# Block 0 of a four-layer kernel: V begun with one token tile on half the contraction, its weights loaded by quarters, two token tiles turned by DMA

## The chip, the cores and the metric

The kernel runs on one core of one Trainium2 chip. The metric is the device time of one execution in microseconds. "PE" is the TensorE matmul queue.

## The reference, cut to what matters

Four layers run in sequence on x (2048 tokens by 1024): attention, gated MLP, attention, gated MLP, each with a LayerNorm before it and a residual. An attention token looks at itself and at seven tokens at distances 2, 4, ... 14. The arithmetic is bf16.

```python
x = x + _A_ref(_layernorm(x), A_wqkv, A_wo)          # S = 2048, D = 1024, 32 heads
x = x + _B_ref(_layernorm(x), B_W_gate, B_W_up, B_W_down)   # F = 3584, relu(gate) * up
x = x + _A_ref(_layernorm(x), A_wqkv, A_wo)
x = x + _B_ref(_layernorm(x), B_W_gate, B_W_up, B_W_down)
```

The kernel works in blocks of 512 tokens, four token tiles of 128 each. Block 0's first stage is the one at issue: load x, normalise it, transpose it (the kernel's matmuls take the dimension that is summed over on the partitions, so normalised x is wanted with the 1024 channels there, as eight chunks `kc` of 128), and multiply by the V weights, then by the Q and K weights. At the start of the program TensorE has nothing to do until the first x and the first weights are there.

## The kernel before: what the change touches

V of block 0 is computed chunk by chunk of its output channels. Each accumulation runs over the whole contraction (`kc` 0 to 7), first for the tokens of tiles 0 and 1 and later for tiles 2 and 3. So the first matmul group needs a slab of V weights of 1 MB that spans all of the contraction.

```python
def v_first(ln):
    plan = [(c, 0, 2) for c in range(6)] + [(c, 2, 4) for c in range(6)] + [(c, 0, 4) for c in range(6, KC)]
    ...
            acc = psum.tile([P, BLK], F32, tag="acc", name="acc_v")
            for kc in range(KC):
                mm(acc[:, cols], lhsT=slab[("v0", c // 4)][:, kc, (c % 4) * P:(c % 4 + 1) * P],
                   rhs=ln["xnT"][:, t0:t1, kc, :], start=(kc == 0), stop=(kc == KC - 1))
            ...
            if i in ln["later"]:
                ln["later"][i]()        # PE transposes of tiles 2 and 3, inside V
```

All four tiles are transposed on TensorE, eight 128 by 128 transposes each, and copied from PSUM, the memory into which the matmuls write:

```python
hold["later"] = {2: (lambda: (turn(2), copy(2, "a", 0), copy(2, "v", 1))),
                 4: (lambda: (turn(3), copy(3, "v", 0), copy(3, "a", 1)))}
```

Nearly every transfer goes through one helper, and each is told to follow the one before it, so SyncE issues them in program order. If one of them has to wait, for data or for a free buffer, all that come after it wait too (in the profile before, the queue stood so once for 6.8 us):

```python
def sp_dma(dst, src, transpose=False):
    start = nc.sync.dma_start_transpose if transpose else nc.sync.dma_start
    if tail_sp[0] is None:
        tail_sp[0] = start(dst, src).ins
    else:
        with tc.issue_after(tail_sp[0]):
            tail_sp[0] = start(dst, src).ins
```

Weights come as slabs of 1 MB into a ring of five buffers, in the order V, V, Q, Q, K, K for block 0. A Q slab and a K slab each hold half of the contraction for all output chunks, so the first K product needs both K slabs. The sixth slab, the second one of K (called "the second K slab" below), must wait until the first V slab's buffer is free. Block 0's Q and K products alternate:

```python
QK_FIRST = [(nm, c) for c in range(KC) for nm in ("q", "k")]
```

## Time and profile before

| | before |
|---|---|
| time, median of 3 | 1619.28 us (1619.16 to 1619.67) |
| first V matmul | 9.83 us |
| first Q matmul of block 0 | 24.67 us |
| first Q matmul of block 1 | 52.30 us |
| gate's first matmul (the first MLP) | 191.08 us |

The span in the profile is about 1.7 us shorter than the time. First the page of the kernel before: span, busy times, and the chain that ended last.

```profile
span 1617.5 us, 18722 instructions
PE 1608.1 (99%) x7505; PEld 784.1 (48%) x7554; DVE 1138.3 (70%) x963; ACT 475.8 (29%) x971; POOL 176.1 (11%) x164
...
PE 99%; DMA 0%; issue 0%; SPq 0%; DVE 0%; DVEq 0%
```

TensorE is busy 99% of the span and the chain is made of it. What could be won is at the two ends. The wait table of PE, before (waiter, what it waited for, us in total, times, longest):

```profile
PE scratch L132 <- DVE ones L290: 1.5, 1, 1.5
PE acc_v L132 <- DMA w_v<-in_A_wqkv_dram: 0.9, 1, 0.9
PE tp L358 <- DVE xn_first L106: 0.7, 1, 0.7
PE tp L358 <- DVE mean L106: 0.4, 1, 0.4
```

These four are all that the table lists for PE, and they lie before the first V matmul. ("scratch" is a set of matmuls on a tile of ones that fills the start.) The chain of waits of the kernel before, in order of time (start, us, what), shows what the first V matmul hangs on:

```profile
2.20 7.59 DMA w_v<-in_A_wqkv_dram
...
9.83 2.79 PE acc_v L132 x24
```

The first V slab was issued at 2.20 us and landed at 9.79; from there on the chain is PE alone. The timeline of PE, before (start, us, engine, line, operation, output<-inputs, count, idle before):

```profile
9.83 2.79 PE L132 MATMUL acc_v<-xnT_first,w_v 128*128 128x256 bf16 x24 [0.86 <-DMA w_v<-in_A_wqkv_dram]
...
24.67 1.89 PE L132 MATMUL acc_q<-xnT_first,w_qk_q 128*128 128x512 bf16 x8
26.40 1.89 PE L132 MATMUL acc_k<-xnT_first,w_qk_k 128*128 128x512 bf16 x8
...
52.30 10.95 PE L132 MATMUL acc_q<-xnT_a,w_qk_q 128*128 128x512 bf16 x50
```

The K products begin with the group at 26.40 us. Its fifth matmul, the first to need the second K slab, is due half a group later, at about 27.26 us, and in the trace that slab landed at 26.83. So 0.4 us of slack was there. Last, the transfers in one-microsecond windows, before (window, PE busy and matmuls, granted clock, mean busy share of the DMA engines, GB/s):

```profile
13.00:14.00 1.00, 1.00 (x12) 1.00 1.04 383
14.00:15.00 1.00, 1.00 (x15) 1.00 1.06 389
15.00:16.00 1.00, 1.00 (x14) 1.00 1.04 385
16.00:17.00 1.00, 1.00 (x12) 1.00 1.06 389
```

While weights stream in, the core moves 381 to 389 GB/s without a break (12 to 19 us). The DMA engines are the second resource of this stretch, and they are full: their mean busy share in these windows is 1.02 to 1.08.

### The profile page before, as it was taken

Reading aid. Unit: us, or ns where it says so; the run is one execution under the profiler, and the core shown is the slowest. Engines: PE = TensorE matmul, PEld = TensorE weight load, DVE = VectorE, ACT = ScalarE, POOL = GpSimd, SP = SyncE. Lnnn points to the kernel's source line nnn. Section 1 sums busy time; section 2 is a strip of 40 time slices with the busy share of each in tenths; the row PEclk is TensorE's granted clock in tenths of the full one; section 3 lists DMA queues with packets and bytes.
Section 4 is the critical chain, followed back from the end, with each engine's and each line's share of the span. In section 5 each row is a group of like instructions: output and inputs, shape, how many; then the busy total and the mean of one; then the engine's idle time right before and its main releaser. Section 6 shows DMA issues by size and latency. Waiting matters only on the chain.

```text
span 1617.5 us, 18722 instructions
## 1 busy us (share of the span) xinstructions
PE 1608.1 (99%) x7505; PEld 784.1 (48%) x7554; DVE 1138.3 (70%) x963; ACT 475.8 (29%) x971; POOL 176.1 (11%) x164
## 2 busy tenths in 40 slices
PE   9999999999999999999999999999999999999999
PEld 6646544444444445444454444544445444444444
DVE  6999979996989698929489293893939939311211
ACT  4853311131116313603136031361313311131110
POOL 2300100010003002300053000530005100000000
PEclk9999999999999999999999999999999999999999
DMA  9868867697669767794747948479574884755452
GB/s 295 184 197 251 213 173 244 182 213 206 209 189 216 202 183 216 188 248 144 229 160 202 240 152 230 153 203 254 160 231 155 207 240 156 209 171 167 155 169 66
DMA packets 408440, 317.92 MB, mean 197 GB/s; under 512 B 166432, under 2 KB 389024, under 8 KB 407840
## 3 DMA queue, kind: packets, MB, share of 16 engines
q1 hardware_dynamic: 407776, 316.13, 69.4%
q8 instruction: 59, 0.97, 0.2%
q10 hardware_dynamic: 576, 0.59, 0.1%
q14 instruction: 29, 0.24, 0.1%
HBM read 266.29 MB, written 34.66 MB: 186 GB/s over the span
## 4 chain that ended last, share of the span: by engine, by line
PE 99%; DMA 0%; issue 0%; SPq 0%; DVE 0%; DVEq 0%
PE acc_u L132 24%; PE acc_g L132 24%; PE dacc L132 18%; PE acc_v L132 7%; PE acc_q L132 7%; PE acc_k L132 7%; PE acc_wo L132 7%; PE dacc_pair L132 6%; DMA w_v<-in_A_wqkv_dram 0%; PE tp L358 0%; SPq L121 0%; PE L L132 0%; DVE x L778 0%; SPq L118 0%; DVEq L1017 0%
## 5 line engine op out<-in xcount | busy, mean ns | idle before, releaser
L132 PE MATMUL acc_g<-xnT_b,w_g 128*128 128x512 bf16 x1792 | 423.3, 379 | 0.0
L132 PE MATMUL acc_u<-xnT_b,w_u 128*128 128x512 bf16 x1792 | 423.3, 379 | 0.0
L731 ACT ACTIVATE r<-acc_g 128x512 bf16<-128x512 f32 x224 | 133.6, 596 | 728.7 <-PE acc_g L132 703.8
L106 DVE TENSOR_TENSOR hT<-acc_u,r 128x512 bf16<-128x512 f32 x224 | 151.0, 687 | 243.3 <-PE acc_u L132 240.8
L132 PE MATMUL dacc<-w_d,hT 128*128 128x512 bf16 (+1 forms) x1372 | 300.4, 375 | 1.5
L132 PEld LDWEIGHTS <-hT 128*128 128x128 bf16 x1820 | 178.1, 98 | 209.0
L132 PEld LDWEIGHTS <-w_g 128*128 128x128 bf16 x1792 | 175.4, 98 | 211.4
L132 PEld LDWEIGHTS <-w_u 128*128 128x128 bf16 x1792 | 175.3, 98 | 211.4
L106 DVE TENSOR_TENSOR pv<-a,vhm 128x4096 bf16<-128x4096 bf16 x64 | 143.6, 2285 | 0.0
L778 DVE TENSOR_TENSOR x<-dacc,x 128x512 bf16<-128x512 f32 (+1 forms) x38 | 24.5, 673 | 154.1 <-PE dacc L132 154.1
L549 DVE TENSOR_TENSOR t<-q,k 128x2048 f32<-128x2048 bf16 x56 | 128.0, 2292 | 6.7 <-ACT k L485 4.6
L106 DVE TENSOR_TENSOR t<-q,k 128x2048 f32<-128x2048 bf16 x56 | 127.5, 2287 | 3.9 <-ACT k L485 2.4
L106 DVE TENSOR_TENSOR pv<-pv 128x1024 bf16<-128x1024 bf16 (+1 forms) x128 | 113.8, 952 | 0.0
L132 PE MATMUL acc_wo<-w_o,oT 128*128 128x512 bf16 x498 | 111.1, 379 | 0.7
L249 POOL TENSOR_TENSOR st_b<-st_b,neg_half 128x1 f32<-128x1 f32 x29 | 43.8, 1517 | 609.9 <-ACT st_b L248 609.9
L562 DVE TENSOR_TENSOR ac<-ac,t 128x2048 f32<-128x2048 f32 x48 | 109.7, 2285 | 0.3
L106 DVE TENSOR_TENSOR ac<-ac,t 128x2048 f32<-128x2048 f32 x48 | 109.7, 2285 | 0.0
L490 POOL COPY kh<-k 128x14 bf16<-128x14 bf16 x40 | 53.7, 1348 | 506.5 <-ACT k L485 410.4
L132 PE MATMUL dacc_pair<-w_d,hT 128*128 128x512 bf16 x413 | 95.5, 379 | 0.4
L132 PEld LDWEIGHTS <-oT 128*128 128x128 bf16 x512 | 50.1, 98 | 60.4
L244 ACT ACTIVATE xn_b<-x 128x1024 bf16<-128x1024 bf16 x29 | 30.3, 1047 | 128.6 <-DVE x L106 66.5
L410 ACT CAST vT<-acc_v 128x512 bf16<-128x512 f32 x56 | 32.7, 586 | 54.0 <-PE acc_v L132 54.0
(131 smaller groups left out, 1226.8 us busy)
## 6 DMA issues: line engine op xcount, KB each, us to landing
w_g<-in_B_W_gate_dram SPq DMA_DIRECT2D x56, 1024.0 KB, 7.2
w_u<-in_B_W_up_dram SPq DMA_DIRECT2D x56, 1024.0 KB, 5.5
w_d<-in_B_W_down_dram SPq DMA_DIRECT2D x48, 1024.0 KB, 6.0
w_o<-in_A_wo_dram SPq DMA_DIRECT2D x16, 1024.0 KB, 6.6
vhm<-v_d SPq DMA_DIRECT2D x32, 284.0 KB, 6.7
v_d<-vT SPq DMA_DIRECT2D x8, 1024.0 KB, 9.0
oT<-o_d SPq DMA_DIRECT2D x32, 256.0 KB, 4.5
w_d<-in_B_W_down_dram SPq DMA_DIRECT2D x16, 512.0 KB, 3.7
```

Source lines behind the costliest of these rows:

```text
L106: tail_dve[0] = f(*args, **kwargs).ins
L132: tail_pe[0] = nc.tensor.matmul(*args, **kwargs).ins
L244: nc.scalar.activation(xn, xt[:], ACT.Square, accum_out=sq)
L249: nc.gpsimd.tensor_tensor(rstd, vpe, neg_half[:, 0:1], op=ALU.pow)
L410: tail_act[0] = nc.scalar.copy(st["vT"][:, c, :], acc[:]).ins
L490: nc.gpsimd.tensor_copy(khalo[n][:, c, :], k[:, BLK:BLK + HALO])
L549: nc.vector.tensor_tensor(t[:], i0, i1, op=ALU.mult)
L562: nc.vector.tensor_tensor(o, ac[:], t[:], op=ALU.add)
L731: tail_act[0] = nc.scalar.activation(rs[j][:], acc[:], ACT.Relu).ins
L778: run = dv if n < NB - 2 else (lambda f, *args, **kwargs: f(*args, **kwargs))
```

## The change

Its intent is to start V earlier. V's first products take tile 0 alone and the first half of the contraction, so they need one tile of x and 1 MB of weights that comes in two quarters on two queues, ahead of x tile 3. Then V is widened: tile 1 on the first half, tiles 0 and 1 on the second half, and the same for tiles 2 and 3. The transposes of tiles 2 and 3 leave TensorE and go through the DMA. To make room, block 0 computes the first Q chunks before the first K chunk (q0 q1 q2 k0 q3 k1 ...), which brings K two groups (3.46 us) later. The diff, cut to its core (the LayerNorm statistics are dealt out anew among the engines, not shown):

```diff
+    def wv_half(hh):
+        return wqkv_v[:, hh * (KC // 2):(hh + 1) * (KC // 2), 2 * D:3 * D]
+
+    def load_slab(key, src):
+        ...
+        if key[0] == "v0":
+            for i in range(2):
+                rows = slice(i * (KC // 4), (i + 1) * (KC // 4))
+                if key[1] == 0 and i == 1:
+                    nc.scalar.dma_start(tv[:, rows, :], src[:, rows, :])
+                else:
+                    sp_dma(tv[:, rows, :], src[:, rows, :])
+        else:
+            sp_dma(tv, src)
@@ LayerNorm of block 0
-        hold["later"] = {2: (lambda: (turn(2), copy(2, "a", 0), copy(2, "v", 1))),
-                         4: (lambda: (turn(3), copy(3, "v", 0), copy(3, "a", 1)))}
+        def turn_dma(t):
+            return lambda: sp_dma(hold["xnT"][:, t, :, :], xna[:, t, :], True)
+        hold["turns"] = [turn_dma(2), turn_dma(3)]
@@ V of block 0
+        def head():
+            for kc in range(KC // 2):
+                if kc == KC // 2 - 1:
+                    ln["second"]()          # tile 1: PE transposes and copies
+                for c in range(KC):
+                    prod(kc, c, 0, 1)       # 128 x 128 times 128 tokens
+        ...
+        tail = [(GRP * (2 + 4 * part + 0.5 * i), second_half(i, 2 * part)) for part in range(2) for i in range(KC // 2)]
+        return head, [(GRP, first_half(1)), (4 * GRP, first_half(2)), (5 * GRP, first_half(3))] + tail
@@ Q and K
-        order = QK_FIRST if n < NB else QK_ORDER
+        order = QK_STAGED if staged else QK_ORDER
@@ order of events
-    ev.append((0.35, lambda: load_x(1)))
+    ev.append((0.05, lambda: load_x(0, [TPB - 1])))
+    ev.append((0.25, head))
+    spread(ln_a[0]["turns"], 0.26, 0.01)
+    ev.append((0.35, lambda: load_x(1, [0, 1])))
+    ev.append((0.45, lambda: load_x(1, [2, 3])))
@@ later events follow the K order, by two groups
-    ev.append((t_v2 + 3.2 * GRP, lambda: head_mm(0)))
+    ev.append((t_v2 + 5.2 * GRP, lambda: head_mm(0)))
```

The place of the two DMA transposes in SyncE's order is behind the first Q slab, ahead of the second Q slab, the x tiles of block 1 and both K slabs.

More of the change, by code (lines that the diff above doesn't have):

```diff
@@ L169, with load_x @@
         x_tiles.append(xt)
-    def load_x(b):
-        for t in range(b * TPB, (b + 1) * TPB):
+    def load_x(b, tiles=range(TPB)):
+        for t in (b * TPB + i for i in tiles):
             if t == 0:
@@ L179, in load_x @@
                 sp_dma(x_tiles[t][:], x_dram[t * P:(t + 1) * P, :])
-    load_x(0)
+    load_x(0, range(TPB - 1))
     slab = {}
@@ L192, in want_v, with want_v_first @@
             want((key, g), wqkv_v[:, :, 2 * D + g * SLAB:2 * D + (g + 1) * SLAB], mid if g == 0 else end)
+    def wv_half(hh):
+        return wqkv_v[:, hh * (KC // 2):(hh + 1) * (KC // 2), 2 * D:3 * D]
+    def want_v_first(end0, end1):
+        for hh, end in enumerate((end0, end1)):
+            want(("v0", hh), wv_half(hh), end)
     def want_qk(key, q_end, k_end):
@@ L213, in want_down @@
             want(("d", n, half, s), wd_v[:, rows, half * SLAB:(half + 1) * SLAB], at + gap * min(8 * (s + 1), FC))
+    def load_slab(key, src):
+        shp = list(src.shape)
+        t = wring.tile([P, 8 * SLAB], BF16, tag="slab", name="w_" + "_".join(str(k) for k in key))
+        tv = t[:, 0:shp[1] * shp[2]].rearrange("p (a b) -> p a b", b=shp[2])
+        if key[0] == "v0":
[7 more added lines that the diff above has]
+            sp_dma(tv, src)
+        slab[key] = tv
     def slab_events(events):
         for i, (key, src, _) in enumerate(slab_plan):
-            def f(key=key, src=src):
-                shp = list(src.shape)
-                t = wring.tile([P, 8 * SLAB], BF16, tag="slab", name="w_" + "_".join(str(k) for k in key))
-                tv = t[:, 0:shp[1] * shp[2]].rearrange("p (a b) -> p a b", b=shp[2])
-                sp_dma(tv, src)
-                slab[key] = tv
+            if key in slab:
+                continue
             ends = sorted(end for _, _, end in slab_plan[:i])
-            events.append((ends[i - RING] + 0.3 if i >= RING else 0.1 * i, f))
+            events.append((ends[i - RING] + 0.3 if i >= RING else 0.1 * i, lambda key=key, src=src: load_slab(key, src)))
     def ln_steps(n, which, early=False, dve=()):
@@ L287, in ln_dve_stats @@
         return mv, rstd
+    load_slab(("v0", 0), wv_half(0))
     ones = const.tile([P, SLAB], BF16, name="ones")
@@ L313, in small @@
             return stat_pool.tile([P, 1], F32, tag="f" + name, name=name, bufs=bufs)
-        mean, vpe, rstd, bst = {}, {}, {}, {}
+        mean, rstd, bst, sq = {}, {}, {}, {}
         def bn(t, half):
@@ L324, in aggr @@
             on("v", nc.vector.bn_aggr, mv[:], bst[t][:].rearrange("p a b -> p (a b)"))
-            vpe[t], mean[t] = small("vpe1"), mv[:, 0:1]
-            on("v", nc.vector.tensor_scalar, vpe[t][:], mv[:, 1:2], EPS, None, op0=ALU.add)
-            power(t)
-        def power(t):
-            rstd[t] = small("rstd1")
-            on("g", nc.gpsimd.tensor_tensor, rstd[t][:], vpe[t][:], neg_half[:, 0:1], op=ALU.pow)
-        def act_stats(t):
-            st1 = stat_pool.tile([P, 2], F32, tag="st1", name="st1")
-            on("a", nc.scalar.activation, xna[:, t, :], x_tiles[t][:], ACT.Identity, accum_out=st1[:, 0:1])
-            on("a", nc.scalar.activation, xna[:, t, :], x_tiles[t][:], ACT.Square, accum_out=st1[:, 1:2])
-            return st1
@@ L339, in act_vpe, with power, act_square @@
-        def act_vpe(t, st1):
+            mean[t] = mv[:, 0:1]
+            power(t, mv[:, 1:2], 1.0)
+        def power(t, var, sign):
+            rstd[t], vpe = small("rstd1"), small("vpe1")
+            on("g", nc.gpsimd.tensor_scalar, vpe[:], var, sign, EPS, op0=ALU.mult, op1=ALU.add)
+            on("g", nc.gpsimd.tensor_tensor, rstd[t][:], vpe[:], neg_half[:, 0:1], op=ALU.pow)
+        def act_square(t):
+            sq[t] = small("sq1")
+            on("a", nc.scalar.activation, xna[:, t, :], x_tiles[t][:], ACT.Square, scale=float(D) ** -0.5,
+               accum_out=sq[t][:])
@@ L340, in act_vpe, with act_mean, act_power @@
+        def act_mean(t):
             mn = small("mean1")
-            on("v", nc.vector.tensor_scalar, mn[:], st1[:, 0:1], 1.0 / D, None, op0=ALU.mult)
+            on("a", nc.scalar.activation, xna[:, t, :], x_tiles[t][:], ACT.Identity, scale=1.0 / D, accum_out=mn[:])
+            mean[t] = mn[:]
+        def act_power(t):
             nvar = small("nvar1")
-            on("v", nc.vector.scalar_tensor_tensor, nvar[:], st1[:, 0:1], mn[:], st1[:, 1:2], op0=ALU.mult, op1=ALU.subtract)
-            vpe[t], mean[t] = small("vpe1"), mn[:]
@@ L345, in act_vpe, with apply @@
-            on("v", nc.vector.tensor_scalar, vpe[t][:], nvar[:], -1.0 / D, EPS, op0=ALU.mult, op1=ALU.add)
-            power(t)
-        def apply(t):
-            on("v", nc.vector.tensor_scalar, xna[:, t, :], x_tiles[t][:], mean[t], rstd[t][:],
+            on("v", nc.vector.scalar_tensor_tensor, nvar[:], mean[t], mean[t], sq[t][:], op0=ALU.mult, op1=ALU.subtract)
+            power(t, nvar[:], -1.0)
+        def apply(t, half=None):
+            cols = slice(0, D) if half is None else slice(half * SLAB, (half + 1) * SLAB)
+            on("v", nc.vector.tensor_scalar, xna[:, t, cols], x_tiles[t][:, cols], mean[t], rstd[t][:],
@@ L354, in turn @@
         def turn(t):
-            tps[t] = [psum.tile([P, KC // 2, P], BF16, tag="acc", name=f"tp{h}") for h in range(2)]
+            if t == 0:
+                tps[t] = [psum.tile([P, KC // 2, P], BF16, tag="acc", name=f"tp{h}")[:] for h in range(2)]
+            else:
+                both = psum_l.tile([P, 2, KC, P], BF16, tag="L", name="tp_pair")
+                tps[t] = [both[:, h, 0:KC // 2, :] for h in range(2)]
             for c in range(KC):
@@ L362, in copy @@
             f = nc.vector.tensor_copy if eng == "v" else nc.scalar.copy
-            on(eng, f, hold["xnT"][:, t, h * (KC // 2):(h + 1) * (KC // 2), :], tps[t][h][:])
+            on(eng, f, hold["xnT"][:, t, h * (KC // 2):(h + 1) * (KC // 2), :], tps[t][h])
+        def turn_dma(t):
+            return lambda: sp_dma(hold["xnT"][:, t, :, :], xna[:, t, :], True)
         warm = small("warm")
         on("a", nc.scalar.activation, warm[:], ones[:, 0:1], ACT.Identity)
-        scratch(14)
+        scratch(13)
         bn(0, 0)
@@ L370, in ln_first, with second @@
         aggr(0)
+        act_square(2)
         bn(1, 0)
+        apply(0, 0)
+        apply(0, 1)
+        turn(0)
+        copy(0, "a", 0)
         bn(1, 1)
         aggr(1)
-        st1 = act_stats(2)
-        apply(0)
-        turn(0)
-        apply(1)
-        copy(0, "a", 1)
-        copy(0, "a", 0)
-        turn(1)
-        act_vpe(2, st1)
-        copy(1, "v", 0)
-        copy(1, "a", 1)
-        bn(3, 0)
-        bn(3, 1)
-        apply(2)
-        aggr(3)
-        apply(3)
-        hold["later"] = {2: (lambda: (turn(2), copy(2, "a", 0), copy(2, "v", 1))),
-                         4: (lambda: (turn(3), copy(3, "v", 0), copy(3, "a", 1)))}
+        copy(0, "v", 1)
+        apply(1, 0)
+        apply(1, 1)
+        act_mean(2)
+        act_power(2)
+        def second():
+            turn(1)
+            copy(1, "v", 0)
+            copy(1, "v", 1)
+            apply(2)
+            act_square(3)
+            act_mean(3)
+            act_power(3)
+            apply(3)
+        hold["second"] = second
+        hold["turns"] = [turn_dma(2), turn_dma(3)]
         return hold
@@ L416, in v_first @@
         st = att[0]
-        plan = [(c, 0, 2) for c in range(6)] + [(c, 2, 4) for c in range(6)] + [(c, 0, 4) for c in range(6, KC)]
-        def f_(i, c, t0, t1):
-            def f():
-                if i == 0:
-                    st["vT"] = big_tile([P, KC, BLK], "vT_0", True)
-                acc = psum.tile([P, BLK], F32, tag="acc", name="acc_v")
-                cols = slice(t0 * P, t1 * P)
-                with pe_group():
-                    for kc in range(KC):
-                        mm(acc[:, cols], lhsT=slab[("v0", c // 4)][:, kc, (c % 4) * P:(c % 4 + 1) * P],
-                           rhs=ln["xnT"][:, t0:t1, kc, :], start=(kc == 0), stop=(kc == KC - 1))
-                tail_act[0] = nc.scalar.copy(st["vT"][:, c, cols], acc[:, cols]).ins
-                if i in ln["later"]:
-                    ln["later"][i]()
-            return f
@@ L434, in v_first, with prod @@
-        at, out = 0.0, []
-        for i, (c, t0, t1) in enumerate(plan):
-            out.append((at, f_(i, c, t0, t1)))
-            at += GRP * (t1 - t0) / TPB
-        return out
+        pairs, opened = {}, set()
+        def prod(kc, c, t0, t1):
+            part = t0 // 2
+            if (part, c // 2) not in pairs:
+                pairs[part, c // 2] = psum.tile([P, 2, BLK // 2], F32, tag="acc", name="acc_v")
+            acc = pairs[part, c // 2][:, c % 2, (t0 % 2) * P:(t0 % 2 + t1 - t0) * P]
+            with pe_group():
+                mm(acc, lhsT=slab["v0", kc // (KC // 2)][:, kc % (KC // 2), c * P:(c + 1) * P],
+                   rhs=ln["xnT"][:, t0:t1, kc, :], start=(part, c // 2) not in opened, stop=(kc == KC - 1),
+                   skip_group_check=True)
+            opened.add((part, c // 2))
@@ new lines, in head, with first_half, second_half, f @@
+        def head():
+            st["vT"] = big_tile([P, KC, BLK], "vT_0", True)
+            for kc in range(KC // 2):
[3 more added lines that the diff above has]
+                    prod(kc, c, 0, 1)
+        def first_half(t):
+            def f():
+                for c in range(KC):
+                    for kc in range(KC // 2):
+                        prod(kc, c, t, t + 1)
+            return f
+        def second_half(i, t0):
+            def f():
+                for c in (2 * i, 2 * i + 1):
+                    for kc in range(KC // 2, KC):
+                        prod(kc, c, t0, t0 + 2)
+                tail_act[0] = nc.scalar.copy(st["vT"][:, 2 * i:2 * i + 2, t0 * P:(t0 + 2) * P],
+                                             pairs.pop((t0 // 2, i))[:]).ins
+            return f
@@ L447 @@
     khalo = {}
-    QK_FIRST = [(nm, c) for c in range(KC) for nm in ("q", "k")]
+    QK_STAGED = [(nm, c) for c in range(KC) for nm in ("q", "k")]
     QK_ORDER = [("q", 0), ("q", 1)]
@@ L855 @@
     t_gu0 = t_fill + GRP * (4 * KC - ahead)
-    want_v("v0", t_v0 + GRP * 5, t_qk0)
+    want_v_first(t_v0 + GRP * 6, t_qk0)
     want_qk("qk01", t_qk1 + GRP * KC, t_v1)
@@ L861 @@
     want_wo(0, t_fill, t_fill)
-    for at, f in v_first(ln_a[0]):
-        ev.append((t_v0 + at, f))
-    ev.append((0.35, lambda: load_x(1)))
-    ev.append((t_v0 + GRP * 5 + 0.6, lambda: load_x(2)))
-    ev.append((t_v0 + GRP * 5 + 0.7, zero_v))
+    head, steps = v_first(ln_a[0])
+    place(steps, t_v0)
+    ev.append((0.05, lambda: load_x(0, [TPB - 1])))
[3 more added lines that the diff above has]
+    ev.append((0.45, lambda: load_x(1, [2, 3])))
+    ev.append((t_v0 + GRP * 6 + 0.6, lambda: load_x(2)))
+    ev.append((t_v0 + GRP * 6 + 0.7, zero_v))
     stats, apply, turn, ln_a[1] = ln_steps(1, "a", True, range(TPB))
@@ L874 @@
     spread(qk_steps(0, ln_a[0], "qk01"), t_qk0, GRP)
-    spread(prod_sum_steps(0), t_qk0 + 3.5, 4.4)
+    spread(prod_sum_steps(0), t_qk0 + GRP * K_STEP[0] + 1.8, 4.4)
     spread(load_v_steps(0), t_qk0 + 19.0, 1.0)
@@ L885 @@
     spread(v_steps(2, ln_a[2], "v123", True), t_v2, GRP)
-    ev.append((t_v2 + 3.2 * GRP, lambda: head_mm(0)))
-    spread(softmax_steps(0), t_v2 + 3.3 * GRP, 0.01)
-    t_pv0 = t_v2 + 2.2 * GRP + 10.0
+    ev.append((t_v2 + 5.2 * GRP, lambda: head_mm(0)))
+    spread(softmax_steps(0), t_v2 + 5.3 * GRP, 0.01)
+    t_pv0 = t_v2 + 4.2 * GRP + 10.0
     spread(pv_steps(0), t_pv0, 4.3)
```

## The prediction

> **What bounds the kernel now.** TensorE. The page gives PE 1608.1 us busy of 1617.5, and the chain that ended last is 99% PE. The wait table shows four PE waits: 1.5 us for the warm-up operand, 0.7 and 0.4 us before the transposes of tiles 0 and 1, 0.9 us for the first V weights. From the first useful matmul (9.83 us) PE runs without a gap worth naming. So a change in block 0 can gain only by starting V earlier or by taking PE work out of the stretch from 9.83 us to the first Q matmul (24.67 us); it can lose by opening a gap.
>
> **What sets 9.83 us.** The first V weights, issued at 2.20 us, land at 9.79: 1 MB behind 1 MB of x in one queue, at 350 to 390 GB/s.
>
> **What the change does.**
> 1. V needs only x of tile 0 and the first half of the contraction (1 MB, in quarters on two queues, ahead of x tile 3). By the one-microsecond windows, the 1.8 MB needed have moved near 7.9 us. [...] The LayerNorm path (statistics end 5.03, two GpSimd operations of about 0.57 us, half applies of 0.3 us, four transposes, a 0.59 us copy) gives xnT's first half near 7.7 us. V starts at about 7.9 us.
> 2. V costs 4 x 1.8 us (32 matmuls of 128 columns at 56 ns, the spacing of the transposes in the trace) plus 2 x 3.45 us (256 columns at 109 ns): 14.1 us against 13.8. The transposes of tiles 2 and 3 (0.9 us) leave PE; tile 1's (0.45 us) move inside V.
> 3. New waits. Tile 1's transposes stand in PE order and wait for its apply (about 9.65 us): 0.4 us. Tiles 2 and 3 go by DMA: a DMA transpose lands 3.1 to 3.8 us after issue on a quiet queue, later behind weights. I expect tile 2 at 15 to 16 us (needed at 15.9), tile 3 at 17.5 (needed at 17.7): 0 to 0.7 us.
>
> Sum: 7.9 + 14.55 + 0.4 + 0.3 = 23.15 us to the first Q matmul, against 24.67: 1.5 us won.
>
> **Kept or lost later?** The new Q/K order brings K chunk 0 two groups (3.46 us) later; the VectorE chain moves with it, and so does the score matmul. VectorE has no idle worth naming from 36 to 184 us, so it loses 3.46 us of slack against PE: before, the last block-0 transpose for the gate stage lands near 187.5 us and gate starts at 191.08, 3.6 us of slack. I allow 0.1 us of loss.
>
> **Prediction:** 1617.8 us, range 1616.6 to 1619.3. Faster by over 2%: 0.005; within 2%: 0.99; slower: 0.005.
>
> **What would show it.** First V matmul near 7.9 us; a PE gap under 0.6 us at tile 1's transposes; 128-column V matmuls 56 ns apart; first Q near 23.2 us; gate's first matmul near 189.6 us with no idle before it.
>
> **What would make it wrong.** DMA transposes landing after 18 us; the second K slab (about 28.1 us, needed about 29) late; VectorE late at the score matmul or at gate, where slack is under 0.5 us; the weights quarter on the second queue late.

V's start of 7.9 us rests on the bytes in the one-microsecond windows of the kernel before and on the LayerNorm path. What the trace of the kernel before shows is that x tiles 1 and 2, issued on two queues at 1.26 and 1.25 us, landed at 4.73 and 4.95. That V's two quarters, on two queues, would land as early as the bytes alone say (near 7.9 us) was the estimate.

## The result

| | before | after |
|---|---|---|
| time, median of 6 | 1619.34 us (1619.16 to 1619.81) | 1619.94 us (1619.55 to 1620.90) |
| first V matmul | 9.83 | 8.37 |
| first Q matmul of block 0 | 24.67 | 23.78 |
| second K slab landed | 26.83 | 30.54 |
| first Q matmul of block 1 | 52.30 | 52.22 |
| gate's first matmul | 191.08 | 191.01 |

The ratio of after to before is 1.0004, with a 95% interval of 0.9991 to 1.0017: the same, and not the 1.5 us faster that was predicted. A ratio here is the mean time of one kernel's fast runs over that of the other's in the same rounds, so it isn't quite the ratio of the medians. The time lies above the predicted range, which ended at 1619.3.

The page of the kernel after:

```profile
span 1618.0 us, 18848 instructions
...
PE 98%; DMA 1%; issue 0%; DVE 0%; SPq 0%; DVEq 0%
```

The DMA now has a share of the chain. The wait table of PE, after:

```profile
PE scratch L132 <- DVE ones L310: 1.5, 1, 1.5
PE acc_v L132 <- DMA w_v<-in_A_wqkv_dram: 0.6, 1, 0.6
PE acc_k L132 <- DMA w_qk_k<-in_A_wqkv_dram: 0.6, 1, 0.6
PE acc_v L132 <- DMA xnT_first<-xn_first: 0.4, 1, 0.4
```

Two waits are gone (those for the transposes of tiles 0 and 1) and two are new, both for transfers: one for the DMA transposes, and one for K weights. The chain of waits, after:

```profile
1.74 6.58 DMA w_v<-in_A_wqkv_dram
...
8.37 1.51 PE acc_v L132 x24
...
11.61 5.04 DMA xnT_first<-xn_first
...
16.70 3.76 PE acc_v L132 x64
...
20.48 10.06 DMA w_qk_k<-in_A_wqkv_dram
...
30.59 1.08 PE acc_k L132 x4
```

Before, the chain left the DMA at 9.79 us for good. Now it comes back to it twice. The last time, PE's V products free a ring buffer at 20.46, the second K slab is issued at 20.48 and lands 10.06 us later, and PE goes on at 30.59. The timeline of PE, after:

```profile
8.37 1.51 PE L132 MATMUL acc_v<-xnT_first,w_v 128*128 128x128 bf16 x24 [0.63 <-DMA w_v<-in_A_wqkv_dram]
...
10.17 6.12 PE L132 MATMUL acc_v<-xnT_first,w_v 128*128 128x128 bf16 x72
16.70 7.24 PE L132 MATMUL acc_v<-xnT_first,w_v 128*128 128x128 bf16 x96 [0.41 <-DMA xnT_first<-xn_first]
23.78 5.34 PE L132 MATMUL acc_q<-xnT_first,w_qk_q 128*128 128x512 bf16 x24
28.96 1.03 PE L132 MATMUL acc_k<-xnT_first,w_qk_k 128*128 128x512 bf16 x4
30.59 1.08 PE L132 MATMUL acc_k<-xnT_first,w_qk_k 128*128 128x512 bf16 x4 [0.60 <-DMA w_qk_k<-in_A_wqkv_dram]
...
52.22 10.96 PE L132 MATMUL acc_q<-xnT_a,w_qk_q 128*128 128x512 bf16 x50
```

The idle times in brackets understate the loss, because the ends of matmuls are modelled: a group of eight is shown with 1.89 us, though the next one starts 1.73 us after it. Counted in starts of matmuls, there are three waits. The products on tile 1 were due at 10.62 us and began at 10.85, 0.23 late, because VectorE was still copying tile 1's transposes out of PSUM (the first of its two copies ended at 10.79; no bracket shows this wait). The products on tile 2 were then due at 16.124 and began at 16.698, 0.57 late. The K group's fifth matmul was due at 29.82 (28.96 plus half a group of 1.73) and began at 30.59, 0.77 late. The sum is then:

- V begins 1.46 us earlier (9.83 to 8.37).
- V takes 0.57 us longer up to the first Q matmul (14.84 to 15.41). Waits make up 0.80 of its time: 0.23 for tile 1's copies and 0.57 for tile 2. So 0.89 us is won at the first Q matmul.
- The wait for the second K slab takes 0.77 of that back, and 0.04 goes in small steps. At block 1's first Q matmul 0.08 us is left (52.30 to 52.22).
- From there on PE runs alike: gate at 191.01 against 191.08 with no idle before it, and the last matmul group starts 0.04 us earlier than before (1613.01 against 1613.05).

The profiled span is nonetheless 0.44 us longer, and that is the last store of the output: in the trace it took 2.17 us to land (at 1616.86) against 1.61 us (at 1616.24). No edit of the change is at that store, but it does not look like chance: over all fourteen profiles it took 2.17 to 2.33 us in the six kernels that have both a quarter of V on ScalarE's queue and tiles 2 and 3 moved by SyncE (after, a0, e2, e3, b2, c2), and 1.56 to 1.61 us in the other eight. Why is not shown.

The windows show why the second K slab was late. After, the same columns as before:

```profile
13.00:14.00 1.00, 1.00 (x12) 1.00 3.12 209
14.00:15.00 1.00, 1.00 (x11) 1.00 0.02 2
15.00:16.00 1.00, 1.00 (x11) 1.00 0.52 112
16.00:17.00 1.00, 0.59 (x9) 1.00 1.38 295
```

Where before had 383 to 389 GB/s, the rate fell to 2 GB/s for a microsecond (a packet is counted in the window in which it starts). Over 13 to 19 us the core moved 1.13 MB (209, 2, 112, 295, 168 and 346 GB/s for a microsecond each) instead of the 2.33 MB that six microseconds at 388 GB/s would have brought: 1.2 MB less, or 3.1 us of a full queue. In the same time 0.5 MB of what did move was the two transposed tiles themselves, another 1.35 us. That makes an estimated 4.4 us by which everything behind them in SyncE's order is late. The wait table of SyncE's queue, after (0 to 22 us), names what that queue stood for:

```profile
SPq L121 <- DVE nvar L106: 6.9, 1, 6.9
```

It stood from about 4.7 to 11.6 us for VectorE to finish normalised tile 2 (this ended at 11.58; the table names the small operation after it), with the rest of the weights behind it. Before, the queue stood as long (6.8 us), but for a free ring buffer, with five slabs and the next x tiles already issued. After, only the V weights and one Q slab were issued. Nor did the queue move on at once when tile 2 was ready. SyncE's timeline, after:

```profile
11.61 3.92 SPq L121 DMA_TRANSPOSE xnT_first<-xn_first  x2
15.58 0.57 SPq L121 DMA_DIRECT2D w_qk_q<-in_A_wqkv_dram  x1
```

Issuing the two transposes took 1.36 and 2.30 us of SyncE, where the copies right after took 0.4 to 0.7 us each, so the second Q slab went out only at 15.58. Meanwhile 19 packets of the transposes stood on the DMA engines for 1.7 to 2.1 us each, the last until 15.66, where their median is 18 ns. All seven profiles with transposes on SyncE in this place have 15 to 21 packets that stood for 0.5 to 2.3 us.

### The profile page after: what moved, and what is told of

Read it like the earlier page. It is cut to its first block, busy times and chain, and to the rows that moved or that the text cites. A ratio compares the mean times of both kernels' runs of the same rounds, so it can differ in the third digit from the quotient of the medians.

```text
span 1618.0 us, 18848 instructions
## 1 busy us (share of the span) xinstructions
PE 1608.2 (99%) x7568; PEld 785.6 (49%) x7617; DVE 1136.3 (70%) x958; ACT 474.5 (29%) x965; POOL 181.1 (11%) x168
## 4 chain that ended last, share of the span: by engine, by line
PE 98%; DMA 1%; issue 0%; DVE 0%; SPq 0%; DVEq 0%
PE acc_u L132 24%; PE acc_g L132 24%; PE dacc L132 18%; PE acc_k L132 7%; PE acc_wo L132 7%; PE acc_q L132 7%; PE acc_v L132 6%; PE dacc_pair L132 6%; DMA w_qk_k<-in_A_wqkv_dram 1%; DMA w_v<-in_A_wqkv_dram 0%; DMA xnT_first<-xn_first 0%; PE L L132 0%; PE tp_pair L383 0%; DVE xnT_first L106 0%; DVE x L829 0%
```

## The experiments

The theory (A) after seeing the trace: the DMA transposes, in the middle of an in-order weight stream, cost that stream time, so the second K slab is late, and PE follows the slab and not V's start. Rivals: (B) the later start of V weights and x tiles, that is the quarters on two queues; (C) the sheer bytes of x tiles 6 and 7, which stand ahead of the second K slab; (D) the new Q/K order with its shifted softmax. The kernels of one group below ran on the same chip, with the same runs of the kernel before.

### First group: which part of the new transfers costs

**a0_after.** The changed kernel unaltered, for the spread.

> The changed kernel again, unchanged. If what the first profile shows is its steady behaviour: first V matmul near 8.4 us, a wait for tile 2 of 0.4 us by the wait table, first Q matmul near 23.8 us, a wait for the second K slab of about 0.6 us (slab landed near 30.5 us), block 1's first Q matmul within 0.3 us of the kernel before (52.30 us), and PE's last matmul within 0.1 us of before. The 0.4 us by which the profiled span was longer than before came only from the landing of the last store (2.19 us against 1.61 us from issue); if that is chance, the span here may fall on either side of before, and the median within 0.6 us of it. Rival: something later in the kernel is really slower, then the last PE matmul is late as well.

Measured: 1619.54 us (1618.85 to 1620.57, 5 runs) against 1619.16 (1619.04 to 1619.75, 9 runs). The profile is of the slowest run, 1620.57: V began at 9.03, because the two first quarters landed at 8.80 and 8.98 (8.14 and 8.33 in the first profile), the first Q matmul was at 24.46, the second K slab landed at 31.46 with a wait of 0.8 us in the table, and block 1's first Q matmul was at 53.14. So the kernel repeats, the K wait is there again, and its start varies by 0.7 us from run to run. That variation is much of the spread of 1.7 us; the kernel before varies by 0.7.

**e1_pe_turns.** Tiles 2 and 3 back on TensorE, everything else as after.

```diff
-        hold["turns"] = [turn_dma(2), turn_dma(3)]
+        hold["turns"] = []
+        hold["pe_turns"] = [turn_pe(2), turn_pe(3)]      # turn(t), then two copies on VectorE
...
+        tail += [(GRP * 2.75, ln["pe_turns"][0]), (GRP * 3.75, ln["pe_turns"][1])]
```

> Undoes one part: tiles 2 and 3 are turned by TensorE again (0.9 us more PE work inside V), the rest of the change stays. Theory (the DMA transposes stop the copies queued around them: rate 0 to 300 GB/s from 13.3 to 18.3 us instead of 385, about 4 us of transfer lost): the rate stays near 385 GB/s, the second K slab lands before 28 us, the waits for tile 2 and for the K slab are both gone; first Q matmul at 23.9 us, block 1's first Q at 51.5 us (0.7 us earlier than changed kernel), total 0.5 to 0.8 us below the changed kernel. Rival (the slab is late because its buffer is freed late, at 20.5 us, or because too many bytes stand in front of it): it still lands near 30 us and the wait of 0.6 us stays, block 1's first Q at 52.2 us or later.

Measured: 1619.34 us (1618.09 to 1621.13, 5 runs) against 1619.16. In the profile (1619.66) both new waits are gone: the second K slab was issued at 21.61, later than in the changed kernel, and landed at 27.57, 3 us sooner. The rate did not dip. But V happened to begin at 9.20 in that run, and PE lost 0.36 us at 248 us to an up-weight slab. From the first V matmul to block 1's first Q matmul PE needed 43.34 us, against 43.85 in the changed kernel and 44.11 in its repeat. So the mechanism (A) holds, and the total did not show it: the start was late and the gain leaked later. That the total would fall was a miss.

**e2_plain_copy.** The two transposes replaced by plain copies of the same bytes. The result is wrong (relative error 0.506).

```diff
-            return lambda: sp_dma(hold["xnT"][:, t, :, :], xna[:, t, :], True)
+            return lambda: sp_dma(hold["xnT"][:, t, :, :].rearrange("p k n -> p (k n)"), xna[:, t, :])
```

> Wrong result on purpose: the two DMA transposes become plain copies of the same 256 KB between the same buffers at the same place in the queue. Theory (transposing, not moving these bytes, opens the hole): no stretch under 300 GB/s between 13 and 18 us, second K slab lands before 28 us, no wait for it, tile 2 no later than 15.9 us; first Q 23.0 to 23.3 us, block 1's first Q near 50.8 us, about 1.4 us before the changed kernel's. Rival (any transfer that waits for the vector engine in this in-order queue starves it): the hole stays, the K slab lands at 30 us, block 1's first Q at 52.2 us.

Measured: 1618.56 us (1618.22 to 1621.18, 4 runs). V began at 7.97 and block 1's first Q matmul came at 50.80, 1.50 earlier than in the kernel before. The second K slab landed at 29.11, just as it was wanted (29.17), and not below 28 as expected. The windows of this kernel:

```profile
13.00:14.00 1.00, 1.00 (x12) 1.00 0.96 344
14.00:15.00 1.00, 1.00 (x12) 1.00 0.71 256
15.00:16.00 1.00, 0.88 (x9) 1.00 0.46 59
16.00:17.00 1.00, 0.95 (x17) 1.00 0.82 252
```

There is a hole with plain copies too: 13 to 19 us lacks 0.62 MB, 1.6 us, half of what the transposes cost. My reading of that half: the first Q slab landed at 14.01, and the second was issued only at 13.50, behind the copy of tile 3, which had waited in the queue for VectorE. Even the first two transfers of the program, with nothing ahead of them, took 2.67 and 2.87 us from issue to landing (x tile 0's halves, in the kernel before), so the stream ran dry. The other half comes with transposing. The trace shows a part of how: issuing the second copy took 0.49 us here, issuing the second transpose 2.30 us in the changed kernel, and the second Q slab went out at 13.50 instead of 15.58. (Tile 2 was also ready 0.41 us sooner here, so the split into halves is rough.) Adding the copies' own bytes (1.35 us) to 1.6 gives 2.95 us. Against c1_pe_one_queue below, where the queue never stopped, the slab is 2.89 us later (29.11 against 26.22); for the changed kernel the estimate of 4.4 stands against 4.32 (30.54 against 26.22). So the sum closes for both kernels.

**e3_x67_late.** x tiles 6 and 7 loaded behind the second K slab.

```diff
-    ev.append((0.45, lambda: load_x(1, [2, 3])))
+    ev.append((t_v0 + GRP * 6 + 0.5, lambda: load_x(1, [2, 3])))
```

> The changed kernel with the loads of x tiles 6 and 7 issued behind the second K slab instead of before it. If bytes in front of the slab decide: it lands 0.52 MB at 385 GB/s = 1.3 us earlier, near 29.2 us, and the wait for it is gone (needed at 29.8 us); block 1's first Q near 51.5 us. But block 1's LayerNorm on the vector engine then ends about 2.7 us later, so the products start 2.7 us later, and I expect that the score matmul waits about 2.5 us: total 1.5 to 2.5 us above the changed kernel. Rival (late buffer release decides when the slab lands): it lands at 30.5 us as before.

Measured: 1618.75 us (1618.60 to 1620.92, 4 runs). Three runs lie between 1618.60 and 1618.87, about 0.8 below the changed kernel's median; the expected 1.5 to 2.5 did not come. So the bytes ahead of the slab (C) are a part of it at most. The profile is of the odd run, 1620.92. PE did not wait for the K slab in it, but this says little, since PE came late itself: the slab landed at 31.01, the first Q matmul was at 25.70. It shows something else. V's first weights landed at 9.49, and PE had stood waiting for 0.7 and then 1.7 us with only eight transposes between, 3.1 us in all. Windows of this kernel:

```profile
9.00:10.00 1.00, 0.46 (x5) 0.50 1.05 408
10.00:11.00 1.00, 1.00 (x12) 0.50 1.06 403
11.00:12.00 1.00, 1.00 (x12) 0.50 1.05 387
12.00:13.00 1.00, 1.00 (x17) 0.81 1.04 383
```

The granted clock fell to 0.50 from 8.97 to 12.38 us. The first 24 V matmuls took 2.53 us instead of 1.35, counted in starts. So a late start can cost a second time.

### Second group: does an earlier start help, and does the cost appear by itself

**b0_before.** The kernel before, unaltered.

> The kernel before, unchanged, profiled a second time. In five profiles of kernels with the changed start, the first half of the V weights landed between 8.3 and 9.7 us, so a V start at 7.9 us was never a fixed value. If the start of the transfers is simply uneven from run to run, V starts here too at a time that differs from 9.83 us by some tenths to one us, and every later stage moves with it. Rival (only the changed kernel's two queues are uneven): V starts at 9.8 us within 0.15 us, and the five times lie within 0.7 us as the earlier runs of before did (1619.0 to 1619.8 us).

Measured: 1619.27 us (1619.08 to 1619.38, 5 runs) against 1619.00 (1618.79 to 1619.93, 9 runs). V began at 9.89 and block 1's first Q matmul was at 52.34, though its first slab landed 0.2 us sooner than in the first profile. The kernel before is steady: its V start waits for the slab and the transposed x alike.

**b1_one_queue.** Both quarters of the first half on SyncE's queue.

```diff
-                if key[1] == 0 and i == 1:
-                    nc.scalar.dma_start(tv[:, rows, :], src[:, rows, :])
-                else:
-                    sp_dma(tv[:, rows, :], src[:, rows, :])
+                sp_dma(tv[:, rows, :], src[:, rows, :])
```

> The changed kernel with the second quarter of the V weights moved from ScalarE's queue to SyncE's, behind the first quarter. Theory (two queues share the rate, so both quarters land together and V waits for the later one): the first quarter lands about 1 us earlier, the second about when it did; V's first matmul at 8.0 to 8.3 us, a small wait in the middle of V's head instead; first Q within 0.3 us of where it stood relative to the landing of the second quarter, the total within 0.5 us of the changed kernel. If instead the two queues are what makes the landing uneven, the five times lie within 0.8 us of each other (changed kernel: 1618.9 to 1620.6 us).

Measured: 1618.78 us (1618.33 to 1619.48, 5 runs) against 1619.00. The quarters landed one after the other, at 7.38 and 8.63 (8.14 and 8.33 on two queues in the changed kernel), and V began at 7.74, 0.63 before the changed kernel's. None of it reached block 1. PE's timeline of this kernel:

```profile
7.74 1.56 PE L132 MATMUL acc_v<-xnT_first,w_v 128*128 128x128 bf16 x24 [0.45 <-ACT xnT_first L325]
...
17.16 7.24 PE L132 MATMUL acc_v<-xnT_first,w_v 128*128 128x128 bf16 x96 [1.39 <-DMA xnT_first<-xn_first]
24.24 5.34 PE L132 MATMUL acc_q<-xnT_first,w_qk_q 128*128 128x512 bf16 x24
...
30.92 1.08 PE L132 MATMUL acc_k<-xnT_first,w_qk_k 128*128 128x512 bf16 x4 [0.47 <-DMA w_qk_k<-in_A_wqkv_dram]
```

The transposed tile 2 landed at 17.12, the second K slab at 30.88, and block 1's first Q matmul was at 52.56, 0.26 later than before. In every run with the new Q/K order in which PE waited for that slab, block 1 began 21.68 or 21.69 us after its landing, whatever V's start:

| run | first V matmul | second K slab landed | block 1's first Q | difference |
|---|---|---|---|---|
| after | 8.37 | 30.54 | 52.22 | 21.68 |
| a0_after | 9.03 | 31.46 | 53.14 | 21.68 |
| b1_one_queue | 7.74 | 30.88 | 52.56 | 21.68 |
| b2_warm | 9.52 | 30.66 | 52.35 | 21.69 |

In the changed kernel the start of V is no longer what sets the time. The slab's landing in turn came 14.8 to 15.2 us after SyncE had issued the second Q slab (at 15.58, 16.27, 16.05 and 15.89 in these four), that is, after it was done with both transposes.

**b2_warm.** Six more scratch matmuls after tile 0's transposes, to keep PE from standing still.

```diff
         copy(0, "a", 0)
+        scratch(6)
         bn(1, 1)
```

> The changed kernel with six more warm-up matmuls (1.3 us) between tile 0's transposes and the first V matmul. In the profiled run of e3_x67_late the granted clock of TensorE was 0.50 from 9 to 12.5 us after TensorE had stood still from 7.7 to 9.5 us, which cost 1.3 us in 24 matmuls. If such drops are what makes the slow executions (1620.5 to 1621.2 us in the changed kernel and its variants), none of the five times here exceeds 1620.3 us and the profile shows clock 1.00 through the first 20 us; V starts no earlier than 8.8 us, so the median is 0 to 0.5 us above the changed kernel's. Rival (slow executions come from late transfers alone): times above 1620.5 us appear here as well.

Measured: 1620.36 us (1619.32 to 1620.45, 5 runs). The clock stayed at 1.00 in the profiled run, and yet three of five runs are at 1620.36 to 1620.45, which the expectation had excluded. V's weights landed late (9.47 and 10.02), and a further 0.55 us went to an up-weight slab at 248 us. So slow executions come from late first transfers as well, and clock drops are not the whole of the spread. What the scratch matmuls themselves do cannot be told from this run.

**b3_turns_only.** The kernel before, with the transposes of tiles 2 and 3 by DMA and nothing else.

```diff
-        hold["later"] = {2: (lambda: (turn(2), copy(2, "a", 0), copy(2, "v", 1))),
-                         4: (lambda: (turn(3), copy(3, "v", 0), copy(3, "a", 1)))}
+        def turn_dma(t):
+            return lambda: sp_dma(hold["xnT"][:, t, :, :], xna[:, t, :], True)
+        hold["later"] = {}
+        hold["turns"] = [turn_dma(2), turn_dma(3)]
...
+    spread(ln_a[0]["turns"], 0.26, 0.01)
     ev.append((0.35, lambda: load_x(1)))
```

> The kernel before with one part of the change alone: tiles 2 and 3 turned by DMA, at the same place in the queue (behind the first Q slab). Theory: the hole of some 4 us in the copies appears here too, at 13 to 18 us; V's second half of tokens, wanted at 15.0 us, waits until the transposes land near 18 us (a wait of 2.5 to 3.5 us), and the K slabs land 3 us later than before, but then V is late as well. First Q at 26.5 to 27.5 us, total 2 to 3.5 us above before. Rival (the transposes by DMA are harmless and only unload TensorE): no new wait, first Q at 23.9 us, total 0.9 us below before.

Measured: 1621.65 us (1621.44 to 1621.72, 4 runs) against 1619.00, a ratio of 1.0015 with an interval of 1.000 to 1.003. The piece alone costs 2.65 us in an otherwise unchanged kernel, although it takes 0.9 us of transposes off TensorE. The matmul on the transposed tiles was due at 14.79 us and began at 17.09 (2.14 in the wait table), the clock was 0.50 from 17.70 to 21.11, and the second K slab landed at 29.99 instead of 26.83. PE itself was so late that it did not have to wait for that slab (wanted at 30.04). So this run shows the slab's lateness by itself, but its own loss came from the wait for the tiles and from the clock.

### Third group: undo, and undo together

**c1_pe_one_queue.** e1 and b1 together: tiles 2 and 3 on TensorE, V's quarters on one queue.

> The version that the runs so far point to: the changed kernel with tiles 2 and 3 turned by TensorE (as e1_pe_turns) and both first quarters of the V weights on one queue (as b1_one_queue). In five profiles block 1's first Q came 21.68 us after the landing of the second K slab whenever PE waited for that slab, whatever V's start (7.7 to 9.5 us). Theory: without the transposes in the queue the slab lands by 27.6 us, before it is wanted, so PE no longer waits for it and the early V start counts: V starts at 7.8 us, first Q at 23.3 to 23.6 us (15.5 us of V work, tile turns included), block 1's first Q at 50.9 to 51.3 us, 1.0 to 1.4 us before the kernel before; total 0.5 to 1.2 us below before. Rival (slab is held by its buffer, freed near 20 us): a wait of some tenths of a us remains and block 1's first Q comes at 51.6 us or later.

Measured: 1618.17 us (1617.77 to 1618.26, 5 runs) against 1619.07 (1618.85 to 1619.25, 9 runs), the two sets of runs apart from each other. V began at 7.65, the first Q matmul at 23.59, the rate stayed at 383 to 395 GB/s through 12 to 19 us, and the second K slab, issued at 20.29, landed at 26.22 (issued at 20.48 and landed at 30.54 in the changed kernel). Block 1 began at 51.22, 1.08 before the kernel before. Part of it leaked later; PE's timeline of this kernel:

```profile
247.42 1.90 PE L132 MATMUL acc_u<-xnT_b,w_u 128*128 128x512 bf16 x8 [0.27 <-DMA w_u<-in_B_W_up_dram]
```

At that point PE is only 0.64 us ahead of the kernel before.

Here are the four combinations side by side, as medians against the kernel before of the same rounds:

| | two queues for V's quarters | one queue |
|---|---|---|
| tiles 2 and 3 by DMA | 0.38 above (a0) | 0.22 below (b1) |
| tiles 2 and 3 on TensorE | 0.18 above (e1) | 0.90 below (c1) |

By the profiles, about 0.6 of a0's excess is the longer last store, which the other three do not have. So neither step alone shows a gain beyond that one, and both together do: e1 kept the late start (V at 9.20) and b1 kept the late slab. The second queue, rival (B), is therefore a part of the cause beside (A). The left pair ran on another chip than the right pair, and only c1's runs lie wholly below those of the kernel before.

**c2_old_order.** The old alternating Q/K order in the changed kernel.

```diff
-        order = QK_STAGED if staged else QK_ORDER
+        order = QK_STAGED if n < NB else QK_ORDER
```

> The changed kernel with one part undone: block 0 takes the old Q/K order (q0, k0, q1, k1, ...). Theory (the second K slab's landing, near 30.5 us or 21 us before block 1's Q, is what PE follows): K chunk 0 is wanted 3.46 us earlier, near 26.4 us, so the wait for the slab grows from 0.6 to 4 us and block 1's first Q comes 3.3 to 3.5 us later than in the changed kernel (near 55.6 us); total 1622.5 to 1623.5 us. The score matmul then waits for nothing. Rival (the order matters little because the vector engine sets the pace): block 1's first Q within 1 us of the changed kernel's.

Measured: 1625.55 us (1624.39 to 1626.87, 4 runs). The slab landed at 30.86, as in the other kernels with DMA transposes, but PE wanted it 3.46 us sooner and stood for 3.9 us. Then the clock was 0.50 from 32.27 to 35.68, and block 1 began at 57.69. The size was missed (1622.5 to 1623.5 was expected): the half clock and a late start of V (9.43) were not in the sum. The direction settles rival (D): the new order doesn't cost, it hides about 3.5 us of the slab's lateness.

**c3_act_turns.** The DMA transposes issued by ScalarE, so that SyncE's order isn't held up.

```diff
-            return lambda: sp_dma(hold["xnT"][:, t, :, :], xna[:, t, :], True)
+            def f():
+                with tc.issue_after(last["a"]):
+                    last["a"] = nc.scalar.dma_start_transpose(hold["xnT"][:, t, :, :], xna[:, t, :]).ins
+            return f
```

> The changed kernel with the two DMA transposes issued by ScalarE instead of SyncE, so that the weights' queue never waits for tiles 2 and 3. It splits the hole: e2_plain_copy showed that about half of it stays with plain copies (the in-order queue ran dry while SyncE waited for the vector engine), so here that half goes and only what transposing itself costs stays. Expected: the second K slab lands 1.5 to 2.5 us earlier than in the changed kernel (28 to 29 us), no wait for it or under 0.2 us; tile 2 turned by 15.9 us or within 0.8 us of it; block 1's first Q 0.4 to 0.9 us before the changed kernel's. Rival (transposing alone makes the hole): the slab lands at 30 us or later and the wait stays.

Measured: 1628.60 us (1626.34 to 1629.86, 4 runs), the worst of all; the expectation failed entirely. The first transpose was issued at 12.75 us and landed at 25.70, 12.95 us later, about when the copies that SyncE had issued before it landed (the first K slab at 24.47, x tile 6 at 25.01). PE waited 8.3 us, and the clock was 0.50 from 21.75 to 28.58. Another queue gave it no way past the backlog. The two queues took turns: from 18 to 23 us, 841 packets of the transposes started, of 256 bytes each, and 783 of the copies, of 2048 bytes each, so the transposes got about 12% of the bytes. The second transpose also held ScalarE, which issued it, from 14.38 to 20.48.

### Fourth group: where the rest of the gain leaks

**d1_up_slab_first.** c1, with the fifth up-weight slab of the first MLP issued ahead of block 1's score loads.

```diff
-            events.append((ends[i - RING] + 0.3 if i >= RING else 0.1 * i, lambda ...
+            early = 1.5 if key == ("u", 0, 4) else 0.0
+            events.append((ends[i - RING] + 0.3 - early if i >= RING else 0.1 * i, lambda ...
```

> c1_pe_one_queue with one slab of up weights (the fifth of block 0) issued ahead of the four loads of block 1's scores instead of behind them. In c1_pe_one_queue PE was 1.08 us ahead of the kernel before until 247 us, then waited for this slab (landed 247.37 us) and was 0.65 us ahead afterwards. Theory: the slab is late because it stands in the in-order queue behind loads that wait for the vector engine, which the new Q/K order made later by two groups relative to PE. Then here it lands before 244 us, PE keeps its 1.1 us to the last matmul, and the total is 0.3 to 0.5 us below c1_pe_one_queue, near 1617.8 us (1.2 to 1.5 us below before). The scores land 1 to 3 us later; the vector engine has idle time there, so this should cost nothing. Rival (its buffer is freed too late): it lands as before and 0.4 us are lost again; or the later scores delay the vector engine and open a new PE wait after 250 us.

Measured: 1617.79 us (1617.75 to 1618.41, 5 runs) against 1619.12 (1618.88 to 1619.64, 9 runs). The slab landed at 239.44 instead of 247.37, and the wait is gone. PE's timeline of this kernel at the same place:

```profile
247.06 1.89 PE L132 MATMUL acc_u<-xnT_b,w_u 128*128 128x512 bf16 x8
```

PE's 1.00 us lead now lasts to its last matmul group. By its medians d1 is 1.3 us below the kernel before and 1.9 us below the changed kernel (relative to the before of each one's own rounds: 1.33 below against 0.60 above; 0.6 of the 1.9 is the last store, 1.57 us here), with a ratio to before of 0.9992 (0.9978 to 1.0006). It is the best version found. It keeps V's early start and the Q/K order, and drops the DMA transposes and the second queue.

## Why the prediction was wrong, point by point

- **What bounds the kernel, and where the gain must come from: right.** PE was the chain, and the chance of a change over 2% was put at 1%.
- **V's start (step 1): right mechanism, size off by 0.47 us.** Predicted 7.9, measured 8.37 (9.03 in the repeat). In the trace, two quarters on two queues landed together, at 8.14 and 8.33 (0.2 to 1.4 us apart in the other seven profiles with two queues), while V needs one of them first. On one queue (b1) they landed at 7.38 and 8.63, and V began 0.63 us sooner. I had counted bytes, but not asked which quarter comes first.
- **V's work (step 2): right.** 128-column matmuls came 56 ns apart.
- **The wait for tile 1 (step 3): 0.4 predicted, 0.23 measured, and in another place.** Its transposes did not wait, but the products after them waited for the copies out of PSUM, which the prediction had left out. **The waits for tiles 2 and 3: 0 to 0.7 predicted, 0.57 measured for tile 2,** which landed at 16.65 and not at 15 to 16; tile 3 landed at 17.58 (17.5 predicted) and was not waited for. The first Q matmul was at 23.78 instead of 23.15: 0.47 of the start, 0.27 of tile 2 beyond the 0.3 allowed, less 0.17 of tile 1, and 0.06 of small steps.
- **"Kept or lost later?" failed, and it is the step that decides.** "The second K slab (about 28.1 us, needed about 29) late" was named as a danger, with 0.9 us of slack. The slab landed at 30.54 and was wanted at 29.82. The 28.1 came from the old queue with its order changed. The term that was mis-sized is what the DMA transposes cost the queue behind them: I entered them only as waits of PE (0 to 0.7 us) and put 0 for the stream, where an estimated 4.4 us belonged (a hole of 3.1 us and their own bytes, 1.35 us). e1, e2 and b3 show in their traces that the slab is late with the transposes and not without: they take them out, replace them, and add them alone. The identity of 21.68 us shows that the slab, and not V, then set block 1. In the total, the gain came back only when the second queue was undone as well (c1).
- **The K order and VectorE's slack: right.** K moved by two groups, gate ran at 191.01 with no idle before it, and the last transposed tile for it landed at 189.71 (187.50 before), 1.3 us ahead. c2 shows that without the new order the loss would have been some 3.5 us larger, and more with the clock drop that followed PE's wait there (0.50 from 32.27 to 35.68 us).
- **The range: too narrow.** It ended 0.02 us above the median of the kernel before as given, and the changed kernel spreads over 1.7 us where the other spreads over 0.7. The repeated median lies 0.4 to 0.6 above before's, while the one trace has PE level with it. The last store would account for that: it took about 0.6 us longer in both profiles of the changed kernel. V's first weights, which landed 0.7 us later in one profile than in the other, add spread. How much each weighs in the timed runs, which have no traces, stays open.

Also open: why packets of the transposes stood for up to 2.1 us in the middle of the stream, why the last store is longer in six of the kernels, and why the first transfers of the program are so uneven (with two queues the earlier of the two first quarters landed anywhere from 7.42 to 9.49 us over eight profiles; with one queue at 7.35 to 7.39 over three).

## What to carry to other kernels

When a queue is in order and full, charge a transfer to whoever stands behind it and not only to its reader: its bytes (1.35 us here, an estimate from 0.5 MB at 388 GB/s), the time for which it waits at the head of the queue (6.9 us), and the hole it leaves in the stream (3.1 us). An earlier start is worth only as much as the next transfer's deadline lets through (here V began 1.46 us earlier, and 0.08 us of it reached block 1), so follow the start to the first operand that the change does not bring forward (here the second K slab) and compute that one's landing anew. Where two operands are late in a row, undoing one of them can show no gain at all (e1 0.18 us above the kernel before, b1 0.22 below) until the other is undone too (c1, 0.90 below). Where the engine that bounds the kernel does a chore in 0.9 us at a known time, moving it into a shared, ordered stream can cost more than it frees (2.65 us in b3).

## What the traces show beside the question

- DMA transposes in a stream of copies: the stretch from 13 to 19 us with two transposes of 0.25 MB carried 1.13 MB (after), with plain copies in their place 1.71 MB (e2), and without either 2.31 MB (c1). A part of this is the queue's wait for VectorE, which the plain copies had too. In the microsecond in which nearly all packets were those of the transposes (16 to 17 us, 1152 of 1159), the rate was 295 GB/s.
- Standstills of PE and the granted clock: it fell to 0.50 after standstills of about 0.7 and 1.7 us with eight transposes between (e3, 3.1 us in all), of 2.14 us (b3), of 3.9 us (c2) and during one of 8.3 us (c3). In c2, standstills of 0.3 and 2.2 us with eight transposes between, before V, left the clock at 1.00. The drop lasted 3.41 us in e3, b3 and c2 alike, and twice that, 6.83 us, in c3. What sets it off is not shown.
- Spacing of matmuls: in V of the changed kernel, where each matmul of 128 columns has a weight load of its own, they came 56 ns apart.
